# The ones beside the values written by GpSimd in place of ScalarE, in the opening of a one-core transformer block

## The chip, the cores and the metric

The kernel runs on one core of one Trainium2 chip. The metric is the device time of one execution in microseconds (us), measured as medians over several runs. All timed runs quoted here are in the fast state (granted TensorE clock 0.998 to 1.0), except one single run (e8) whose state is unknown and which is used for its trace alone. Where a ratio is quoted, it is the mean time of one kernel's fast runs over the mean of the other's fast runs of the same rounds, so it is not quite the ratio of the medians.

The engines are called TensorE (PE in the profile, PEld for its weight loads), VectorE (DVE), ScalarE (ACT) and GpSimd (POOL); SP issues most of the transfers.

## The reference

A block of 2048 rows by 512 columns: attention with 32 heads of 16, then a gated unit of width 1792, each behind a layer norm.

```python
x = A_x
h = x + _A_ref(_layernorm(x, axis=-1), A_wqkv, A_wo)
h2 = h + _B_ref(_layernorm(h, axis=-1), B_w_gate, B_w_up, B_w_down)
return h2
```

## The kernel before

The kernel fixes the order of every engine's instructions itself. In the opening it loads the first 512 rows (four row tiles of 128), takes each tile's mean and variance, normalises and transposes them, projects the first queries and keys, and then starts the exponentials, which go on until 696 us. The attention sums come from a column of constants beside each head's 16 values: `Vaug` has 17 columns per head, and the last one must be filled once ("the ones" below; the value written is 0.5). That is 16 row tiles x 32 heads = 512 elements of 2 bytes in each partition, 34 bytes apart. Some names recur: the ramp is a row of the numbers 0 to 31, from which VectorE makes the identity matrix that TensorE transposes with; the masks pick out single heads, and the mask scaling multiplies one of them by a constant; the warming matmuls are products of `fill` that nobody reads, run while TensorE would otherwise wait.

```python
nc.vector.memset(eps_t[:], 1e-5)
nc.scalar.activation(out=A0[:], in_=eps_t[:], func=ACT.Sqrt)      # warms the table
fill = prep.tile([P, QC], BF16, name="fill")
nc.scalar.activation(out=Vaug[:, :, :, DH:VW], ...)               # the ones: 0.5 everywhere
nc.gpsimd.memset(fill[:], 1.0)                                    # for TensorE's warming matmuls
nc.gpsimd.memset(eps4_t[:], 4e-5)
nc.gpsimd.memset(power[:], -0.5)
ramp = prep.tile([P, 2, 32], BF16, name="ramp")
for k in range(32):
    nc.gpsimd.memset(ramp[:, 0, k:k + 1], float(k))               # VectorE makes the identity of it
nc.gpsimd.tensor_scalar(out=eps4_t[:], in0=eps4_t[:], scalar1=1.0, scalar2=None, op0=ALU.mult)
# ... cut: VectorE's identity and masks, then the tasks of the opening
def stats_task(c, i):
    def on_act():      # tile 1: mean and mean square by two activations on ScalarE
        ...
    # tiles 0, 2, 3: ln_stats on VectorE
def root(i):           # ScalarE: square root of the variance
    ...
def pool_rstd(c, i):   # later tiles: GpSimd makes the scale ...
    ...
def pool_apply(c, i):  # ... and the normalised rows that TensorE transposes
    ...
```

The `tensor_scalar` at the end of GpSimd's part multiplies by one: it changes nothing. It stands there so that GpSimd has run such an instruction once before its real work, which begins with the second group of row tiles.

Of the kernel before, what the change touches and what calls it, by code (L numbers as in the profile page):

```python
# [8 lines left out]
FP32 = mybir.dt.float32  # L9
# [6 lines left out]
ACT = mybir.ActivationFunctionType  # L16
# [130 lines left out]
def kernel(  # L147
# [11 lines left out]
    nc = tc.nc  # L159
    P = 128  # L160
    S, D = A_x.shape[1], A_x.shape[2]
    H, DH = 32, 16
    F = B_w_gate.shape[1]
    NT = S // P
# [19 lines left out]
    VW = DH + 1  # L184
# [21 lines left out]
    eps_t = const.tile([P, 1], FP32)  # L206
# [10 lines left out]
    Vaug = const.tile([P, NT, H, VW], BF16)  # L217
# [26 lines left out]
    for c in range(2, NQC):  # L244
# [5 lines left out]
    nc.vector.memset(eps_t[:], 1e-5)  # L250
    nc.scalar.activation(out=A0[:], in_=eps_t[:], func=ACT.Sqrt)
    fill = prep.tile([P, QC], BF16, name="fill")
    nc.scalar.activation(out=Vaug[:, :, :, DH:VW], in_=eps_t[:].to_broadcast([P, NT * H]).rearrange(
        "p (t h o) -> p t h o", t=NT, o=1), func=ACT.Copy, scale=0.0, bias=0.5)
    nc.gpsimd.memset(fill[:], 1.0)
    nc.gpsimd.memset(eps4_t[:], 4e-5)
    nc.gpsimd.memset(power[:], -0.5)
    ramp = prep.tile([P, 2, 32], BF16, name="ramp")
    for k in range(32):
        nc.gpsimd.memset(ramp[:, 0, k:k + 1], float(k))  # L260
    nc.gpsimd.tensor_scalar(out=eps4_t[:], in0=eps4_t[:], scalar1=1.0, scalar2=None, op0=ALU.mult)
    psp = main.enter_context(tc.tile_pool(name="psum", bufs=1, space=PSUM))
    PS = psp.tile([P, 8, QC], FP32, name="PS")
# [149 lines left out]
    for i in range(TQ):  # L413
# [5 lines left out]
            out=mv0[i][:, 2:3], in_=mv0[i][:, 2:3])))  # L419
# [6 lines left out]
    for h in range(2):  # L426
# [5 lines left out]
        out=small.tile([P, 1], FP32, name="warm")[:], in_=eps_t[:], func=ACT.Exp)))  # L432
# [18 lines left out]
    for word in START:  # L451
        t, eng = tasks[word[1:]], word[0]
# [1071 lines left out]
    while chain:  # L1524
# [8 lines left out]
    fill = [lambda i=i: nc.tensor.matmul(hps[i], lhsT=ident2[:], rhs=xl[:, i, :], start=True, stop=False)  # L1533
            for i in range(n)]
    fill += [lambda p=p, i=i: nc.tensor.matmul(hps[i], lhsT=OT[qc, p][:, i * P:(i + 1) * P], rhs=wo_sb[:, p, :],
                                               start=False, stop=False) for p in range(NP - 1) for i in range(n)]
    fill = deque(fill)
    nc.scalar.activation(out=small.tile([P, 1], FP32, name="warm")[:], in_=eps_t[:], func=ACT.Sqrt)
    tw = {}
    for i in range(QB):  # L1540
        t = dvx.tile([P, 3, GQ, QC], I16, name="J", bufs=QB)[:].rearrange("p a b n -> p (a b n)")
# [139 lines left out]
```

## Time and profile before

| | before |
|---|---|
| median of the 6 runs beside the changed kernel | 731.30 us (731.12 to 732.11) |
| span of the profiled run | 729.3 us |
| first large exponential begins | 12.68 us |
| GpSimd's first TENSOR_SCALAR begins | 11.55 us |
| GpSimd's first real work begins | 15.35 us |

The prediction shows the page, the chain of waits and the timeline of the opening. Five more lines of the timeline of the kernel before matter later. The columns of the timeline are start in us, length in us, engine, line, operation, output and input, shapes, count, and in brackets the idle time before it with what ended it.

```profile
4.93 0.89 ACT L364 ACTIVATE junk<-xb 128x512 bf16<-128x512 bf16 x1
...
7.55 0.40 PE L315 MATMUL PS<-ident_bf,xn 128*128 128x128 bf16 x4 [1.11 <-DVE xn L385]
...
12.68 8.36 ACT L1447 ACTIVATE pt<-PS 128x1024 f16<-128x1024 f32 x9 [0.50 <-PE PS L1067]
...
15.35 0.24 POOL L538 TENSOR_SCALAR nv<-mv 128x2 f32<-128x2 f32 x1 [3.54 <-DVE mv L284]
...
43.89 3.28 ACT L1447 ACTIVATE xb<-PS 128x1024 f16<-128x1024 f32 x3 [0.19 <-issue]
```

ScalarE begins the statistics of row tile 1 at 4.93 us, and the first large exponential at 12.68. TensorE waits 1.11 us for the first normalised rows. GpSimd is ready early and waits 3.54 us for VectorE before its first real work: that is its slack. And at 43.89 us ScalarE has a short idle time of 0.19 us that nothing in the profile explains ("issue").

### The profile page before, as it was taken

The page shows a single profiled execution, that of the slowest core. Times are in us where ns is not written, and L with a number is a line of the kernel's source. Part 1 is how long each engine was busy: PE and PEld are TensorE (multiplying, and loading weights), DVE is VectorE, ACT ScalarE, POOL GpSimd, SP SyncE. Part 2 cuts the span into 40 slices and gives each one's busy share as a digit, 9 for nine tenths or more (in the row PEclk, how much of TensorE's full clock was granted, in tenths as well). Part 3 has the DMA queues.
Part 4 walks back from the last instruction along what each step waited for, and adds up shares of the span by engine and source line. Part 5 has one row for each costly group of instructions (what it writes and reads, how often), then busy time and mean ns, then how long its engine had stood idle before and what let it go on. Part 6 is the DMA issues. An engine that isn't in the chain of part 4 may idle for free.

```text
span 729.3 us, 26553 instructions
## 1 busy us (share of the span) xinstructions
PE 712.6 (98%) x11169; PEld 335.7 (46%) x11169; DVE 664.1 (91%) x1299; ACT 702.0 (96%) x787; POOL 426.4 (58%) x728
## 2 busy tenths in 40 slices
PE   8999999999999999999999999999999999999997
PEld 3322224444454445544545454545554455445564
DVE  7989989999999998999999999989999999999952
ACT  8999999999999999999999999999999999999962
POOL 2725657775566755656656766566664665666610
PEclk9999999999999999999999999999999999999999
DMA  8300006000223013211224023301322133013450
GB/s 259 88 11 10 11 8 178 2 3 2 74 78 95 14 33 105 85 45 46 67 62 109 9 82 89 75 17 44 106 67 60 39 103 103 10 24 89 117 161 19
DMA packets 85741, 47.39 MB, mean 65 GB/s; under 512 B 17520, under 2 KB 85616, under 8 KB 85616
## 3 DMA queue, kind: packets, MB, share of 16 engines
q1 hardware_dynamic: 85328, 45.37, 22.1%
q8 instruction: 89, 1.46, 0.9%
q14 instruction: 36, 0.29, 0.1%
q10 hardware_dynamic: 288, 0.26, 0.1%
HBM read 37.75 MB, written 2.10 MB: 55 GB/s over the span
## 4 chain that ended last, share of the span: by engine, by line
PE 69%; ACT 20%; DVE 7%; issue 2%; DMA 1%; POOL 1%; SPq 0%; ACTq 0%; DVEq 0%; POOLq 0%
PE PS L1067 23%; PE PS L1235 20%; ACT pt L1447 13%; PE PS L803 12%; PE PS L821 6%; DVE J L1259 3%; PE PS L321 3%; ACT xnT L1447 2%; PE PS L326 2%; PE PS L746 2%; ACT xb L1447 1%; ACT th L833 1%; ACT QTb L1447 1%; POOL J L1280 1%; DMA out_dram<-ob 1%
## 5 line engine op out<-in xcount | busy, mean ns | idle before, releaser
L1280 POOL INT64_ADD J<-J x658 | 407.9, 632 | 253.5 <-DVE J L1259 207.2
L1447 ACT ACTIVATE pt<-PS 128x1024 f16<-128x1024 f32 (+2 forms) x523 | 519.9, 1117 | 2.9 <-PE PS L1067 2.4
L1259 DVE TENSOR_SCALAR J<-PS 128x512 int16<-128x512 f32 x626 | 411.5, 678 | 17.7 <-PE PS L1067 12.6
L1067 PE MATMUL PS<-QT,KT 32*128 32x256 bf16 (+1 forms) x3712 | 264.1, 276 | 8.6 <-ACT pt L1447 3.6
L1235 PE MATMUL PS<-J,Vaug 128*17 128x256 f16 (+1 forms) x3195 | 226.1, 279 | 0.5 <-DVE J L1304 0.3
L1235 PE MATMUL PS<-pt,Vaug 128*17 128x256 f16 (+1 forms) x2042 | 198.3, 279 | 0.0
L1067 PEld LDWEIGHTS <-KT 32*128 32x128 bf16 x3840 | 89.7, 92 | 204.3 <-issue 200.5
L1235 PEld LDWEIGHTS <-Vaug 128*17 128x17 bf16 x5841 | 131.5, 90 | 78.4 <-issue 73.6
L803 PE MATMUL PS<-xnT,wgu 128*128 128x256 bf16 x784 | 112.9, 275 | 0.0
L1447 ACT ACTIVATE xnT<-PS 128x1024 f16<-128x1024 f32 (+1 forms) x85 | 92.2, 1116 | 0.5 <-PE PS L1067 0.2
L1304 DVE TENSOR_TENSOR J<-J 128x1024 f16<-128x1024 f16 (+1 forms) x110 | 78.4, 713 | 12.7 <-POOL J L1280 12.2
L803 PEld LDWEIGHTS <-wgu 128*128 128x128 bf16 x784 | 63.8, 98 | 38.5 <-issue 32.7
L821 PE MATMUL PS<-wd,hT 128*128 128x512 bf16 x196 | 56.7, 384 | 0.0
L833 ACT ACTIVATE th<-PS 128x512 f32<-128x512 f32 (+1 forms) x63 | 38.8, 616 | 8.8 <-DVE hT L816 5.0
L1235 PE MATMUL PS<-xnT,Vaug 128*17 128x256 f16 x346 | 46.7, 274 | 0.0
L1447 ACT ACTIVATE QTb<-PS 128x1024 f16<-128x1024 f32 x40 | 44.0, 1100 | 0.0
L875 DVE SCALAR_TENSOR_TENSOR hT<-th,PS 128x512 bf16<-128x512 f32 x49 | 33.1, 676 | 0.8 <-PE PS L803 0.8
L1134 DVE STREAM_TRANSPOSE xs<-PS 128x256 f32<-128x256 f32 (+1 forms) x60 | 27.5, 458 | 1.7 <-PE PS L1235 1.4
L1105 DVE TENSOR_TENSOR o<-xs,rsum 128x128 bf16<-128x128 f32 (+1 forms) x60 | 24.5, 409 | 2.1
L1447 ACT ACTIVATE xb<-PS 128x1024 f16<-128x1024 f32 (+1 forms) x25 | 26.0, 1086 | 0.3 <-issue 0.2
L1235 PE MATMUL PS<-QTb,Vaug 128*17 128x256 f16 x160 | 25.7, 274 | 0.0
L1447 ACT ACTIVATE pe<-PS 128x1024 f16<-128x1024 f32 (+1 forms) x21 | 21.9, 1094 | 0.9 <-PE PS L1067 0.8
(126 smaller groups left out, 390.7 us busy)
## 6 DMA issues: line engine op xcount, KB each, us to landing
wgu<-in_B_w_gate_dram SPq DMA_DIRECT2D x49, 256.0 KB, 3.0
wgu<-in_B_w_up_dram SPq DMA_DIRECT2D x49, 256.0 KB, 3.4
out_dram<-ob SPq DMA_DIRECT2D x16, 128.0 KB, 1.7
QT<-qd SPq DMA_DIRECT2D x112, 16.0 KB, 1.8
wd<-in_B_w_down_dram SPq DMA_DIRECT2D x1, 1792.0 KB, 9.2
xr<-in_A_x_dram SPq DMA_DIRECT2D x14, 128.0 KB, 3.4
xb<-in_A_x_dram SPq DMA_DIRECT2D x6, 256.0 KB, 5.5
J<-in_B_w_gate_dram SPq DMA_DIRECT2D x4, 384.0 KB, 4.3
```

The lines of the kernel that those rows point to most:

```text
L803: nc.tensor.matmul(ps[:, 0:PARTS[r][2]].rearrange("p (i q) -> p i q", q=P), lhsT=w[:, d, :], rhs=hn_of(r)[:, :, d, :], start=(d == 0), sto ...
L821: nc.tensor.matmul(ps, lhsT=hT[:, f, i * P:(i + 1) * P], rhs=wd[:, f, :], start=(f == 0), stop=(f == FC - 1))
L833: nc.scalar.activation(out=th[:, 0:ps.shape[-1]], in_=ps, func=ACT.Tanh, scale=0.5)
L875: nc.vector.scalar_tensor_tensor(out=hT[:, f:f + k, 0:w], in0=th[f][:].rearrange("p (k n) -> p k n", k=k), scalar=1.0, in1=ps2.rearrange(" ...
L1067: nc.tensor.matmul(pss[:, ui, i * CW[qc]:(i + 1) * CW[qc]], lhsT=KT[g // 2][32 * j:32 * j + 32, k * P:(k + 1) * P], rhs=q[32 * j:32 * j + ...
L1105: nc.vector.tensor_tensor(out=o2[:, 0:w // 32, DH * a:DH * a + DH], in0=xs[:, 0:w // 32, 0:DH], in1=rec.to_broadcast([P, w // 32, DH]), op ...
L1134: j = dve(650 - ns[0], lambda: nc.vector.transpose(out=xs[:, 0:w // 32, :].rearrange("p b r -> p (b r)"), in_=src), LAST, st["xs"], pr=-1)
L1235: nc.tensor.matmul(dst[32 * j:32 * j + VW, 0:w], lhsT=un.v[:, kt * SPAN[qc] + i, h, :], rhs=un.ap[:, i * w:(i + 1) * w], start=clears and ...
L1259: nc.vector.tensor_scalar(out=J[:, 0, k, :], in0=src, scalar1=ZOFF, scalar2=float(-min(CHORDS)), op0=ALU.add, op1=ALU.max)
L1280: nc.gpsimd.int64_add(words(s), words(0), CHORDS[s - 1] * (1 + 2 ** 16 + 2 ** 32 + 2 ** 48))
L1304: nc.vector.tensor_tensor(out=f1, in0=f1, in1=J[:, 0, 0:k, :].bitcast(FP16), op=ALU.add)
L1447: ex = nc.scalar.activation(out=pt, in_=pss[:, 0:wa, :], func=ACT.Exp, scale=AS)
```

## The change

Its intent: ScalarE shall begin the statistics of row tile 1 as soon as the tile lands, and VectorE its own likewise. GpSimd takes over the ones, behind the ramp that VectorE waits for; and the fill is written as 256 fp32 words with the same bits, to be out of the ramp's way sooner.

```diff
     fill = prep.tile([P, QC], BF16, name="fill")
-    nc.scalar.activation(out=Vaug[:, :, :, DH:VW], in_=eps_t[:].to_broadcast([P, NT * H]).rearrange(
-        "p (t h o) -> p t h o", t=NT, o=1), func=ACT.Copy, scale=0.0, bias=0.5)
-    nc.gpsimd.memset(fill[:], 1.0)
+    nc.gpsimd.memset(fill[:].bitcast(FP32), 1.001937866210938)
     nc.gpsimd.memset(eps4_t[:], 4e-5)
     nc.gpsimd.memset(power[:], -0.5)
     ramp = prep.tile([P, 2, 32], BF16, name="ramp")
     for k in range(32):
         nc.gpsimd.memset(ramp[:, 0, k:k + 1], float(k))
+    nc.gpsimd.memset(Vaug[:, :, :, DH:VW], 0.5)
     nc.gpsimd.tensor_scalar(out=eps4_t[:], in0=eps4_t[:], scalar1=1.0, scalar2=None, op0=ALU.mult)
```

## The prediction

> **What bounds the kernel now.** I first read the page, to see which engine limits the whole run.
>
> ```profile
> PE 712.6 (98%) x11169; PEld 335.7 (46%) x11169; DVE 664.1 (91%) x1299; ACT 702.0 (96%) x787; POOL 426.4 (58%) x728
> PE 69%; ACT 20%; DVE 7%; issue 2%; DMA 1%; POOL 1%; SPq 0%; ACTq 0%; DVEq 0%; POOLq 0%
> ```
>
> The first line is busy time per engine in a span of 729.3 us, the second the chain of work that ended last. The reader is to see a program with TensorE and ScalarE (ACT) full nearly to the end. Such a middle part leaves little to win, and the change touches nothing in it. What it touches lies before the first large exponential (ACT, line 1447, at 12.68 us), so I then read the chain of waits in order of time over the first 24 us. Its columns are start and length in us, and the work.
>
> ```profile
> 1.64 1.28 ACT L251
> 2.92 0.01 issue
> 2.93 0.20 ACT warm L251
> 3.13 2.26 ACT Vaug L253
> 5.40 0.52 ACT junk L364 x2
> 5.92 0.02 issue
> 5.94 0.72 ACT junk L366 x2
> 6.66 0.19 ACT QT L381
> 6.86 0.02 issue
> 6.88 0.17 DVE QT L418
> 7.05 0.03 issue
> 7.08 0.41 DVE xn L385
> ```
>
> The write of the 512 ones (Vaug L253) is on the chain with 2.26 us. It delays ACT's statistics of row tile 1 (L364, L366), these the first square root (L381), and that VectorE's (DVE's) reciprocal (L418) and normalised rows (L385), which everything later waits for. Last I read the timeline of all engines over the same stretch.
>
> ```profile
> 0.73 0.52 POOL L255 MEMSET fill<- 128x512 bf16 x1 [0.29 <-POOLq L1665]
> 1.25 1.12 POOL L260 MEMSET ramp<- 128x1 bf16 x32
> 1.31 5.13 PE L448 MATMUL PS<-fill 128*128 128x512 bf16 x13 [1.31 <-POOL eps_t L256]
> ...
> 2.41 0.21 DVE L266 STREAM_TRANSPOSE ramp<-ramp 128x32 bf16<-128x32 bf16 x1 [1.45 <-POOL ramp L260]
> ...
> 3.71 0.17 DVE L274 TENSOR_SCALAR maskz<-mask 128x2 f32<-128x2 f32 x1
> 3.79 0.69 DVE L281 BATCH_NORM_STATS2 st<-xb 128x6 f32<-128x512 bf16 x1
> ...
> 6.88 0.16 DVE L418 RECIPROCAL QT<-QT 128x1 f32<-128x1 f32 x1 [1.40 <-ACT QT L381]
> ...
> 11.55 0.26 POOL L261 TENSOR_SCALAR eps_t<-eps_t 128x1 f32<-128x1 f32 x1 [9.17 <-issue]
> ```
>
> DVE sits idle for 1.40 us before its first reciprocal, because of ACT; and its first statistics follow its mask work without a gap, 0.08 us after that work's last start. The transfers of the opening, asked for narrow stretches, give issue to landing: tile 0 is issued at 0.73 and takes 3.0 us (lands at 3.73); tile 1 takes 2.8 (3.53); tiles 2 and 3 are issued near 1.2 and take 3.2 and 2.9 (about 4.4 and 4.1). So DVE already starts almost at the landing of tile 0, while ACT starts tile 1 at 4.93, 1.4 us after it landed.
>
> **What the Trainium skill says.** "SBUF — State Buffer", the note on cachelines under "Door 1: The DMA port swizzle": accesses within one 16-byte line go at full rate, each crossing to a new line costs. The ones lie 17 bf16 elements, 34 bytes, apart, so every element is a new line. The trace agrees for ACT: 512 strided elements took 2.36 us, while the same kind of write of 512 elements into a dense PSUM row (line 430) took 0.61. Whether GpSimd (POOL) pays this, no row of before shows. "GPSIMD Engine Reference", section 3.1, gives 1.03 cycles per element for the simplest bodies: 512 x 1.03 / 1.2 GHz = 0.44 us; the trace agrees, 0.46 us from the start of fill's memset to the next start (0.73 to 1.19). Its section 2.1 says that the first call of a freshly loaded kernel hides a load of about 6 us that no row shows; the trace has 9.17 us of "issue" before POOL's first TENSOR_SCALAR, which I read as this, at a different size. "SBUF — State Buffer", section "Who interferes with whom": POOL and DVE share one port pair, which a two-port DVE instruction takes for its whole length; no wait of before's opening shows such a block.
>
> **The change part by part.**
> *Fill as fp32 words.* The 512 bf16 become 256 fp32, the same bits. At 0.46/512 us each, half of them saves 0.23 us of POOL ahead of the ramp. Ramp, DVE's transpose and masks, and TensorE's warming matmuls all come 0.23 earlier. For DVE the statistics cannot come before tile 0 at 3.73: gain there about 0.05 us, to about 3.75. TensorE's 13 fills end near 6.2 in place of 6.44.
> *ACT's write goes.* The warm square root runs from 2.93 to 3.13, tile 1 lands at 3.53, so its statistics begin near 3.56. In the trace, the activation of line 366 needs 0.54 us to its read of the accumulator and 0.63 to the next ACT work; the first pass needs about 0.75 alike (0.54 and the 0.21 from 5.73 to 5.94). So the first root starts at 3.56 + 0.75 + 0.63 = 4.94 in place of 6.57, 1.63 earlier. It needs DVE's statistics of tile 0, done at about 4.65, so it needn't wait. Its result reaches DVE 0.31 later (6.57 to 6.88 now), at 5.25.
> *The next wait.* DVE must by then have finished tile 2, which it takes before the reciprocal: that ends at 5.30 + 0.18 = 5.48 now and about 5.45 after. So the reciprocal starts near 5.45 and not 5.25: DVE gains 6.88 - 5.45 = 1.43 us, its whole idle time and no more. This is the term I choose as the gain.
> *What follows.* The normalised rows start near 5.65; TensorE's transpose, 0.46 later now (7.08 to 7.54), could start at 6.1 but stands behind the fills to 6.2, so it gains about 1.3. Four warming matmuls and the first projection then come near 7.36 (8.65 now); its weights, issued at 1.67 and 2.16 with 4.3 and 4.4 us, land at 6.0 and 6.6, no limit. The second transpose (9.13 now) depends on DVE and can gain the 1.43. ACT's table load for the exponentials, 8.93 now, comes near 7.64 and still ends before the copy that follows needs it. First exponential: about 12.68 - 1.4 = 11.3 us.
> *The memset of the ones.* It starts near 2.15 on POOL, after the ramp. If strides are free it lasts 0.45 us; at ACT's rate 2.3, to 4.4. Its readers come late: the scaling of Vaug (DVE, 15.87 now) and the first products with it (TensorE, 16.87 now).
> *The sum at the end.* Behind the first exponential the order on every engine is unchanged. The later weights wv, wq and wk land at about 9.5, 14.0 and 15.4, well before their uses (wv at 13.44 now, wk's projection at 25.17), so the shift should be passed to the end. I take 1.35 of the 1.43, for a little loss in later waits: 731.24 - 1.35 = 729.89, say 729.9 us.
>
> **The rivals.**
> First, *POOL blocks DVE*: if the memset holds the shared pair until 4.4, the small mask scaling (near 3.5) waits, statistics start near 4.4, tile 2 ends near 6.1, and the gain is 6.88 - 6.1 = 0.8 us: 730.4. For it speaks ACT's own slow strided write; against it, that the mask scaling has two elements and may not use the second port. I give it one chance in five.
> Second, *POOL becomes late*: if the 9.17 us count from the end of the memset, POOL is ready at 4.4 + 9.2 + 0.3 = 13.9 in the slow case. Its first real work starts at 15.35 now, so about 13.95 after: no slack left. In the quick case it is ready near 12.1. A further 1 us here could stall TensorE's transposes of the next rows (18.91 now, about half a us after their rows were written). Then most of the gain would go: 730.5 to 731.2. One chance in ten.
> Third, *the gain is swallowed*: some later transfer or a drift between engines takes up the shift. Against it: TensorE's waits from 12.6 to 700 us sum up to only a few us, nearly all on ACT or DVE, which shift along, and 0.7 us on one transfer that this core issues itself.
> Fourth, *the gain stops at 0.23 us*, the fill alone, if ACT's write was not the limit; the chain above speaks against it.
>
> **Range and chances.** The main line gives 729.9; blocking or a late POOL gives 730.4 to 731; a full gain of 1.6, which would need DVE faster too, gives 729.6. The three runs of before span 0.9 us (731.21 to 732.11), two of them within 0.03. So 729.3 to 730.9 should hold it eight times in ten. Two per cent is 14.6 us, more than the whole opening of 12.7 us: within 2% is all but certain.
>
> **What would show it.** Right: ACT's first statistics near 3.56, DVE's idle before the first reciprocal gone, the first root near 4.94 and reciprocal near 5.45, the first exponential near 11.3, DVE's first statistics at about 3.75, and Vaug off the chain. Wrong: DVE's mask scaling or statistics starting past 4 us beside a long POOL memset (first rival); POOL's TENSOR_SCALAR ending past 14 us, with waits for POOL behind it (second); an early first exponential with an unchanged end (third). The prediction fails above all if the memset is far longer than ACT's 2.4 us, or if the shift is lost behind 12 us.

## The result, and the profile after

The median went from 731.30 to 730.41 us (six runs each; 730.12 to 731.64 after). The ratio is 0.9988 with a 95% interval of 0.9975 to 1.0001: within 2%, and on these runs alone not even clearly apart from no change. The lines below have numbers lower by one in the changed kernel (L1447 is L1446 there).

The page of the changed kernel, the two lines that answer to those of before:

```profile
PE 702.4 (96%) x11111; PEld 335.8 (46%) x11169; DVE 663.9 (91%) x1299; ACT 700.2 (96%) x786; POOL 429.0 (59%) x729
PE 62%; ACT 23%; DVE 6%; issue 4%; DMA 2%; SPq 1%; POOL 1%; DVEq 0%; ACTq 0%; POOLq 0%
```

ScalarE has one instruction fewer (786 for 787) and 1.8 us less work, GpSimd one more and 2.6 us more. TensorE's 10 us less are no gain: 58 matmul records are missing from this trace (11111 for 11169), and the weight loads are all there. The timeline of its opening:

```profile
0.73 0.31 POOL L253 MEMSET fill<- 128x256 f32 x1 [0.29 <-POOLq L1664]
...
2.10 2.27 POOL L259 MEMSET Vaug<- 128x512 bf16 x1
2.20 0.21 DVE L265 STREAM_TRANSPOSE ramp<-ramp 128x32 bf16<-128x32 bf16 x1 [1.24 <-POOL ramp L258]
...
3.41 0.63 ACT L363 ACTIVATE junk<-xb 128x512 bf16<-128x512 bf16 x1 [0.28 <-DMA xb<-in_A_x_dram]
3.51 0.88 DVE L273 TENSOR_SCALAR maskz<-mask 128x2 f32<-128x2 f32 x1
3.60 0.79 DVE L280 BATCH_NORM_STATS2 st<-xb 128x6 f32<-128x512 bf16 x1
...
4.79 0.28 ACT L380 ACTIVATE QT<-QT,eps_t 128x1 f32<-128x1 f32 x1
...
5.34 0.13 DVE L417 RECIPROCAL QT<-QT 128x1 f32<-128x1 f32 x1
...
5.98 0.40 PE L314 MATMUL PS<-ident_bf,xn 128*128 128x128 bf16 x4
...
11.10 3.77 ACT L1446 ACTIVATE pt<-PS 128x1024 f16<-128x1024 f32 x4 [0.50 <-PE PS L1066]
...
14.40 0.37 POOL L260 TENSOR_SCALAR eps_t<-eps_t 128x1 f32<-128x1 f32 x1 [10.04 <-issue]
14.85 0.24 POOL L537 TENSOR_SCALAR nv<-mv 128x2 f32<-128x2 f32 x1
```

ScalarE now waits for the transfer itself and starts at 3.41 us in place of 4.93; VectorE's wait of 1.40 us before the reciprocal is gone, and the reciprocal starts at 5.34 in place of 6.88. The first large exponential starts at 11.10 in place of 12.68, 1.58 us earlier. But GpSimd's TENSOR_SCALAR has moved from 11.55 to 14.40, and its real work follows at 14.85 without the slack of before. Two waits of the changed kernel show what came of it; the first line is from the waits of TensorE between 12 and 40 us (us in total, times, longest), the second from the timeline of ScalarE.

```profile
PE PS L692 <- POOL xn L544: 0.2, 1, 0.2
```

```profile
42.98 3.28 ACT L1446 ACTIVATE xb<-PS 128x1024 f16<-128x1024 f32 x3 [0.50 <-issue]
```

In the kernel before, TensorE had no wait for GpSimd in that stretch, and ScalarE's idle time there was 0.19 us.

To see where the shift is lost, take the 688 activations of 1024 or 1536 columns, which come in the same order in every kernel, and subtract the start of the same one in the trace of before. A negative number is a kernel ahead of it.

| activation (start before) | 1st (12.68) | 11th (21.94) | 26th (38.80) | 31st (45.71) | last (694.82) |
|---|---|---|---|---|---|
| changed kernel | -1.58 | -1.21 | -1.21 | -0.90 | -1.08 |

So the opening gained 1.58 us; 0.37 went by 21.94 us and 0.31 between 38.8 and 45.7 us. After that the shift moves between -1.2 and -0.6 us, and the two traces end 1.08 us apart, against 0.89 us between the medians. The experiments are about the two losses.

One view misleads here. The chain of waits of the changed kernel over its first 24 us runs so:

```profile
7.29 0.04 issue
7.33 7.81 DMA wk_sb<-in_A_wqkv_dram
15.15 0.03 POOLq L544
15.17 0.74 POOL rstd L538
```

It lays GpSimd's lateness on the transfer of `wk_sb`, because an update of that transfer came just before. But L538 reads only what L537 wrote and the constant `power`, and GpSimd's rows stand back to back from 14.40 us on. In e2 below the same instruction starts at 14.29 us, while the transfer lands only near 15.4 there (issued at 7.71, 7.7 us to landing). The releaser is inferred from what ended last, and this one is a coincidence. What held GpSimd is in its own row: 10.04 us of idle time before the TENSOR_SCALAR.

### The profile page after: what moved, and what is told of

Same layout as the page of the kernel before. It is cut to its first block, busy times and chain, and to the rows that moved or that the text cites. A ratio compares the mean times of both kernels' runs of the same rounds, so it can differ in the third digit from the quotient of the medians.

```text
span 728.3 us, 26497 instructions
## 1 busy us (share of the span) xinstructions
PE 702.4 (96%) x11111; PEld 335.8 (46%) x11169; DVE 663.9 (91%) x1299; ACT 700.2 (96%) x786; POOL 429.0 (59%) x729
## 4 chain that ended last, share of the span: by engine, by line
PE 62%; ACT 23%; DVE 6%; issue 4%; DMA 2%; SPq 1%; POOL 1%; DVEq 0%; ACTq 0%; POOLq 0%
PE PS L1066 21%; PE PS L1234 18%; ACT pt L1446 17%; PE PS L802 11%; PE PS L820 5%; DVE J L1258 3%; PE PS L320 3%; ACT xnT L1446 3%; PE PS L325 1%; ACT QTb L1446 1%; DMA wk_sb<-in_A_wqkv_dram 1%; PE PS L745 1%; ACT th L832 1%; ACT xb L1446 1%; PE PS L1640 1%
## 5 line engine op out<-in xcount | busy, mean ns | idle before, releaser
L1446 ACT ACTIVATE pt<-PS 128x1024 f16<-128x1024 f32 (+2 forms) x523 | 519.9, 1115 | 3.1 <-PE PS L1066 2.2
L1066 PE MATMUL PS<-QT,KT 32*128 32x256 bf16 (+1 forms) x3712 | 263.9, 276 | 13.9 <-ACT pt L1446 5.7
L1446 ACT ACTIVATE xnT<-PS 128x1024 f16<-128x1024 f32 (+1 forms) x85 | 92.2, 1117 | 0.4 <-PE PS L1066 0.2
L820 PE MATMUL PS<-wd,hT 128*128 128x512 bf16 x167 | 50.2, 383 | 3.5 <-issue 3.5
L1446 ACT ACTIVATE QTb<-PS 128x1024 f16<-128x1024 f32 x40 | 44.0, 1100 | 0.0
L1446 ACT ACTIVATE xb<-PS 128x1024 f16<-128x1024 f32 (+1 forms) x25 | 26.0, 1084 | 0.6 <-issue 0.5
L1446 ACT ACTIVATE pe<-PS 128x1024 f16<-128x1024 f32 (+1 forms) x21 | 21.8, 1092 | 0.9 <-PE PS L1066 0.8
```

Of the source, the lines that this page charges most:

```text
L820: nc.tensor.matmul(ps, lhsT=hT[:, f, i * P:(i + 1) * P], rhs=wd[:, f, :], start=(f == 0), stop=(f == FC - 1))
L1066: nc.tensor.matmul(pss[:, ui, i * CW[qc]:(i + 1) * CW[qc]], lhsT=KT[g // 2][32 * j:32 * j + 32, k * P:(k + 1) * P], rhs=q[32 * j:32 * j + ...
L1446: ex = nc.scalar.activation(out=pt, in_=pss[:, 0:wa, :], func=ACT.Exp, scale=AS)
```

## The experiments

Eleven runs were made, of nine new kernels, the changed one again and e7 again; all gave correct results. The table has them together, with the shifts as above. "Idle" is the idle time before GpSimd's first TENSOR_SCALAR, "TS" its start.

| kernel | idle | TS | 1st | 11th | 26th | 31st | last | median (runs) | ratio to before |
|---|---|---|---|---|---|---|---|---|---|
| before | 9.17 | 11.55 | 0 | 0 | 0 | 0 | 0 | 731.30 (6) | |
| changed | 10.04 | 14.40 | -1.58 | -1.21 | -1.21 | -0.90 | -1.08 | 730.41 (6) | 0.9988 |
| after_again | 9.67 | 14.03 | -1.52 | -1.52 | -1.53 | -1.22 | -1.70 | 730.42 (5) | 0.9984 |
| e1_fill_only | 8.54 | 10.71 | 0.00 | 0.00 | -0.01 | -0.01 | +0.22 | 731.45 (4) | 1.0000 |
| e2_ones_behind_load | 8.58 | 10.74 | -1.38 | -1.38 | -1.34 | -1.04 | -1.68 | 729.72 (5) | 0.9977 |
| e3_ones_on_dve | 8.45 | 10.61 | -0.96 | -0.96 | -0.97 | -0.66 | -0.37 | 730.84 (5) | 0.9986 |
| e4_mask_late | 11.39 | 15.76 | -1.63 | +0.10 | +0.10 | +0.41 | -0.10 | 731.16 (4) | 0.9990 |
| e5_ones_twice | 9.55 | 16.25 | -0.65 | +0.59 | +0.58 | +0.95 | +1.00 | 732.12 (4) | 1.0004 |
| e6_ones_split | 7.86 | 10.59 | -1.64 | -1.64 | -1.52 | -1.21 | -1.59 | 730.29 (4) | 0.9982 |
| e7_act_count | 8.52 | 10.68 | -1.45 | -1.45 | -1.41 | -1.41 | -1.60 | 729.61 (5) | 0.9970 |
| e8_dense_delay | 12.53 | 17.00 | +0.01 | +1.31 | +1.30 | +1.38 | +1.52 | 732.59 (1) | |
| e9_after_act_count | 9.32 | 13.70 | -1.57 | -1.56 | -1.57 | -1.50 | -1.77 | 729.59 (5) | 0.9973 |
| e10_best_again | 7.60 | 9.76 | -1.65 | -1.65 | -1.60 | -1.52 | -1.91 | 729.21 (6) | 0.9970 |

The kernel before, beside these, had medians of 731.57 (e1, e2, e4, e5), 731.77 (after_again, e3, e6, e7) and 731.53 (e8, e9, e10). All shifts are against the one trace of the kernel before. after_again, e3, e6 and e7 ran on one chip, the other experiments on another.

My theory at the start: ScalarE's write was the limit of the opening, and GpSimd's new work makes it late for TensorE. The rival: something else took the gain, such as a fixed time of GpSimd or drift.

### e1_fill_only: the fill alone

```diff
-    nc.gpsimd.memset(fill[:], 1.0)
+    nc.gpsimd.memset(fill[:].bitcast(FP32), 1.001937866210938)
```

> Only the fill as 256 fp32 words; ScalarE still writes the ones. Theory (ScalarE's write was the limit): VectorE's masks about 0.22 us earlier, but ScalarE's statistics still at about 4.9 us and the first large exponential at 12.6 to 12.7 us, so the end is within 0.1 us of the kernel before (731.3). Rival (the ramp in front of VectorE was the limit): the first exponential about 0.2 us earlier, near 12.45, and the end likewise.

Measured: the first exponential is where it was (shift 0.00), the ratio 1.0000 (0.9985 to 1.0015). Its timeline has VectorE's masks 0.20 us earlier, and ScalarE's first root unmoved:

```profile
3.51 0.17 DVE L274 TENSOR_SCALAR maskz<-mask 128x2 f32<-128x2 f32 x1
...
6.57 0.46 ACT L381 ACTIVATE QT<-QT,eps_t 128x1 f32<-128x1 f32 x2
```

So the fill gives nothing by itself; the opening's gain needs ScalarE's write to go.

### e2_ones_behind_load: the ones behind GpSimd's first TENSOR_SCALAR

```diff
-    nc.gpsimd.memset(Vaug[:, :, :, DH:VW], 0.5)
     nc.gpsimd.tensor_scalar(out=eps4_t[:], in0=eps4_t[:], scalar1=1.0, scalar2=None, op0=ALU.mult)
+    nc.gpsimd.memset(Vaug[:, :, :, DH:VW], 0.5)
```

> The changed kernel with the memset of the ones behind GpSimd's first TENSOR_SCALAR. Theory (the idle time before that instruction counts from the memset's end, and GpSimd's lateness gives back part of the gain): TENSOR_SCALAR at about 2.1 + 9.2 = 11.3 us, memset 11.6 to 13.9, first real GpSimd work near 14.0 in place of 14.85, no wait of TensorE for GpSimd's rows at 18 us, and the shift of the exponentials stays near 1.5 us at 40 us in place of 0.9 to 1.2. The mask scaling takes 0.17 us again in place of 0.88. End about 729.9 to 730.1. Rival (the load comes at a fixed time or the loss behind 12 us is something else): TENSOR_SCALAR still near 14 us or the shift drops to 1.2 us at 20 us as before; end 730.4.

Measured, in its timeline:

```profile
10.74 0.26 POOL L259 TENSOR_SCALAR eps_t<-eps_t 128x1 f32<-128x1 f32 x1 [8.58 <-issue]
10.96 2.27 POOL L260 MEMSET Vaug<- 128x512 bf16 x1
13.96 0.25 POOL L537 TENSOR_SCALAR nv<-mv 128x2 f32<-128x2 f32 x1 [0.74 <-DVE mv L283]
```

The TENSOR_SCALAR comes 8.58 us after the ramp, the memset fits into the hole behind it, and GpSimd waits for VectorE again (0.74 us) in place of the other way round. Nothing is lost between the 1st and the 11th exponential. The time is 729.72 us, the ratio 0.9977 (0.9963 to 0.9990). The first exponential gained only 1.38 here, 0.20 less than in the changed kernel: TensorE's 13 warming matmuls took 5.73 us in this trace and 5.01 in the other, so the first transpose began at 6.62 and not at 5.98. The instructions are the same. The warming matmuls start 0.40 to 0.43 us apart at first; in the changed kernel the last two of the 12 intervals are 0.22 and 0.21, in after_again the last three 0.22 to 0.27, and in e2 none is under 0.40. So when TensorE goes over to its faster rate differed from run to run.

### e4_mask_late: the small mask scaling out of the memset's way

```diff
 def masks():
     nc.vector.tensor_reduce(out=mask[:], ...)
-    nc.vector.tensor_scalar(out=maskz[:], in0=mask[:], scalar1=ZS, scalar2=None, op0=ALU.mult)
...
 def fix(c, i):
     mv = mv0[i]
+    if i == 1:
+        nc.vector.tensor_scalar(out=maskz[:], in0=mask[:], scalar1=ZS, scalar2=None, op0=ALU.mult)
```

> The changed kernel with VectorE's mask scaling (two elements) moved behind the first normalised rows, out of the time of GpSimd's memset. Theory (the small mask scaling takes two ports and waits for the memset, and the statistics end behind it): statistics of tile 0 end near 4.26 in place of 4.39, first reciprocal near 5.2 in place of 5.34, first exponential near 11.0 in place of 11.10; end the same as the changed kernel (730.4), since GpSimd is late all the same. Rival (the statistics themselves are slowed by the memset, or wait for the rows): statistics still end at 4.39 and the reciprocal stays at 5.34.

Measured:

```profile
3.60 0.69 DVE L279 BATCH_NORM_STATS2 st<-xb 128x6 f32<-128x512 bf16 x1
...
5.22 0.13 DVE L418 RECIPROCAL QT<-QT 128x1 f32<-128x1 f32 x1
...
15.76 0.26 POOL L260 TENSOR_SCALAR eps_t<-eps_t 128x1 f32<-128x1 f32 x1 [11.39 <-issue]
```

The next line is from the waits of TensorE between 12 and 45 us.

```profile
PE PS L693 <- POOL xn L545: 1.5, 2, 1.1
```

The statistics end at 4.29 in place of 4.39 and the reciprocal starts at 5.22 in place of 5.34: the block behind the memset is real, and worth 0.12 us there and 0.05 at the first exponential. What I had not expected is the second half: the same memset is followed by 11.39 us of idle time here, TensorE waits 1.5 us for GpSimd's rows, and the whole gain of the opening is gone by the 11th exponential (+0.10). Nothing in this edit touches GpSimd. So the idle time varies from run to run, and the loss with it; the four timed runs spread from 730.17 to 731.44 us.

### e5_ones_twice: the memset doubled

```diff
+    nc.gpsimd.memset(Vaug[:, :, :, DH:VW], 0.5)
     nc.gpsimd.memset(Vaug[:, :, :, DH:VW], 0.5)
```

> The changed kernel with the memset of the ones done twice, same values. Theory (lateness of GpSimd goes to the end nearly one to one): second memset ends at 6.6 us, TENSOR_SCALAR near 16.7 us in place of 14.40, first exponential still at 11.1 us, but TensorE waits some 2.3 us more for GpSimd's rows near 18 to 20 us, end about 732 to 732.7. Rival (GpSimd's time in the opening is hidden): end within 0.3 us of 730.4. Rival (load at a fixed time): TENSOR_SCALAR at 14.4 us as in the changed kernel.

Measured: TENSOR_SCALAR at 16.25 us, and the end 732.12 us, as the theory has it. It was wrong on the first exponential, which gained only 0.65: the second memset also held VectorE.

```profile
4.43 2.28 POOL L260 MEMSET Vaug<- 128x512 bf16 x1
...
5.52 1.33 DVE L385 TENSOR_SCALAR xn<-xb,QT 128x512 bf16<-128x512 bf16 x1
```

The normalising of the first rows, 0.41 us elsewhere, took 1.33 and ended just after the memset did (6.71 us). From the 1st to the 11th exponential another 1.24 us went.

### after_again: the changed kernel once more

No edit.

> The changed kernel itself once more, for a second trace on this chip. Theory (the idle time before GpSimd's first TENSOR_SCALAR varies from run to run, 8.5 to 11.4 us seen so far, and only beyond about 9.3 us does it delay TensorE): that idle time differs from the 10.04 us of the first trace, and the shift of the exponentials at 20 us is about 1.58 less the excess over 9.3 us; times spread by more than 0.5 us. Rival (fixed load): idle time again 10.0 us, shift 1.2 us at 20 us, spread under 0.3 us.

Measured:

```profile
14.03 0.26 POOL L260 TENSOR_SCALAR eps_t<-eps_t 128x1 f32<-128x1 f32 x1 [9.67 <-issue]
```

The idle time is 9.67 us and nothing is lost by the 11th exponential; its five runs span 729.40 to 730.85 us, the ratio is 0.9984 (0.9970 to 0.9998). The same program loses 0.37 us in one trace and nothing in another. The threshold of 9.3 us that I had expected was wrong: by it 0.37 us should have gone here too.

### e3_ones_on_dve: the ones on VectorE, before the ramp arrives

```diff
     nc.vector.memset(ident_bf[:], 0.0)
+    nc.vector.memset(Vaug[:, :, :, DH:VW], 0.5)
...
-    nc.gpsimd.memset(Vaug[:, :, :, DH:VW], 0.5)
```

> The changed kernel with the ones written by VectorE in its idle time before the ramp (0.96 to 2.20 us). Theory (a strided write of 2-byte elements costs every engine near 4.4 ns each, as ScalarE 2.36 us and GpSimd 2.27 us for 512): memset 2.3 us, transposed ramp only at about 3.2 us, statistics from about 4.6 us in place of 3.6, first exponential about 12.0, end about 730.7 to 731.0. Rival (VectorE writes one element per cycle at any stride): memset 0.6 us, hidden; TENSOR_SCALAR of GpSimd near 10.7 us, first exponential near 11.0 to 11.3, end 729.5 to 729.9, as good as the ones behind the load.

Measured:

```profile
2.66 0.48 DVE L264 MEMSET Vaug<- 128x512 bf16 x1 [1.70 <-issue]
2.78 0.39 DVE L265 STREAM_TRANSPOSE ramp<-ramp 128x32 bf16<-128x32 bf16 x1
```

The row says 0.48 us, but 1.70 us of unexplained idle time stand before it, and the profile shows nothing that the memset waits for: VectorE was free at 0.96 us and the row ends at 3.14. If the memset began at 0.96, it took about 2.2 us, 4.3 ns for each element, which is close to GpSimd's 4.4 (2.27 / 512). That is inferred: a memset of 0.48 us that began late for a reason the profile doesn't show would leave the same row. The transposed ramp is done 0.76 us later than in the changed kernel (3.17 for 2.41), and the first exponential gains 0.96 in place of 1.58. The end, 730.84 us, is in the theory's range. Whichever it was, VectorE is no better place.

### e6_ones_split: a quarter of the ones early, the rest behind the load

```diff
-    nc.gpsimd.memset(Vaug[:, :, :, DH:VW], 0.5)
+    nc.gpsimd.memset(Vaug[:, 0:TQ, :, DH:VW], 0.5)
     nc.gpsimd.tensor_scalar(out=eps4_t[:], ...)
+    nc.gpsimd.memset(Vaug[:, TQ:NT, :, DH:VW], 0.5)
```

> The changed kernel with the ones of row tiles 0 to 3 (128 elements) behind the ramp and the other 384 behind GpSimd's first TENSOR_SCALAR. Theory: first part 128 x 4.4 ns = 0.57 us (2.1 to 2.7), over before the mask scaling at 3.5, which takes 0.17 us; TENSOR_SCALAR near 2.7 + 8.6 to 9.3 = 11.3 to 12.0 us; second part 1.7 us, done by 13.8; no wait of TensorE for GpSimd at 18 us; end as with all behind the load, 729.6 to 730.0. Rival (load fixed in time or the memset's length is an overhead per instruction): first part over 1 us, mask scaling blocked, end 730.3.

Measured:

```profile
2.10 0.64 POOL L259 MEMSET Vaug<- 128x128 bf16 x1
10.59 0.26 POOL L260 TENSOR_SCALAR eps_t<-eps_t 128x1 f32<-128x1 f32 x1 [7.86 <-issue]
10.81 1.73 POOL L261 MEMSET Vaug<- 128x384 bf16 x1
```

The time goes with the number of elements, the mask scaling is not held (0.17 us), and the trace loses nothing by the 11th exponential. Its median, 730.29 us, is worse than expected, though the profiled run (729.51) is not; the three timed rounds (730.26 to 730.62) have no trace, so what happened in them stays open.

### e8_dense_delay: GpSimd late, and nothing else changed

This is e1 with a dense memset that nobody needs, of about the same length, while ScalarE still writes the ones.

```diff
+    nc.gpsimd.memset(Vaug2[:, 0:5], 0.5)
     nc.gpsimd.tensor_scalar(out=eps4_t[:], ...)
```

> The kernel before with the fill as fp32 words and one extra dense memset of 2720 2-byte elements (into a tile that is overwritten later) on GpSimd behind its ramp; ScalarE writes the ones. It asks what lengthens the idle time before GpSimd's first TENSOR_SCALAR (8.5 us behind the bare ramp, 9.55 to 11.4 behind the strided memset of the ones). Theory (a later start of it meets the busy transfers of the opening): dense memset 2.4 us, idle again 9.5 us or more, TENSOR_SCALAR past 14 us. Rival (it is the strided memset itself): idle about 8.5 us, TENSOR_SCALAR near 13.1 us. Mask scaling: blocked again (about 0.9 us) if any long memset of GpSimd does it.

Measured:

```profile
2.10 2.37 POOL L261 MEMSET Vaug<- 128x2720 bf16 x1
...
3.51 0.97 DVE L275 TENSOR_SCALAR maskz<-mask 128x2 f32<-128x2 f32 x1
...
17.00 0.26 POOL L262 TENSOR_SCALAR eps_t<-eps_t 128x1 f32<-128x1 f32 x1 [12.53 <-issue]
```

(The profile leaves out the number in `Vaug2`.)

The first exponential is where it was (+0.01), the 11th is 1.31 us late: GpSimd's lateness alone does it. A dense memset (2.37 us for 2720 elements, 0.87 ns each) holds VectorE's mask scaling as the strided one does, and the idle time behind it is the longest of all. So, as far as this one trace tells, it needs no stride to be that long.

The four traces with a loss agree on one rule. Take the start of TENSOR_SCALAR after the first exponential, less what was lost by the 11th: 14.40 - 11.10 - 0.37 = 2.93 (changed), 15.76 - 11.05 - 1.73 = 2.98 (e4), 16.25 - 12.02 - 1.24 = 2.99 (e5), 17.00 - 12.69 - 1.30 = 3.01 us (e8). Up to about 2.95 us after the first exponential GpSimd's first TENSOR_SCALAR is hidden (after_again: 2.88, no loss); beyond that, in these four, each us is lost.

### e7_act_count: one small activation put back on ScalarE

All kernels without ScalarE's write up to here lost 0.30 to 0.37 us between the 26th and the 31st activation, with 0.50 us or more of idle time at the same row; before and e1 did not. What they share is one instruction fewer on ScalarE. So e7 is e2 with a tiny activation in the old place, where ScalarE would wait for its rows anyway.

```diff
     nc.scalar.activation(out=A0[:], in_=eps_t[:], func=ACT.Sqrt)
+    nc.scalar.activation(out=A0[:], in_=eps_t[:], func=ACT.Copy, scale=0.0, bias=0.5)
```

> The ones behind the load, with one small ScalarE activation (128x1) put back where its write of the ones stood, so that ScalarE has as many instructions as before. Theory (the 0.31 us that every kernel without ScalarE's write lost near 43 us, idle time 0.50 in place of 0.19 with no releaser shown, comes from where that instruction stands in ScalarE's stream): idle time 0.19 again and the shift is the same at 38 and at 46 us; end 0.3 us earlier than the ones behind the load, about 729.4. Rival (it comes from absolute time or from other engines): idle time 0.50 again, end 729.7.

Measured:

```profile
42.48 3.28 ACT L1447 ACTIVATE xb<-PS 128x1024 f16<-128x1024 f32 x3 [0.19 <-issue]
```

The idle time is 0.19 us again and the shift is the same at the 26th and the 31st (-1.41). The median is 729.61 us, all five runs lie within 0.45 us (729.25 to 729.70), and the ratio is 0.9970 (0.9956 to 0.9983). An instruction more made the kernel no slower; its median is 0.1 us ahead of e2's where 0.3 was expected, on another chip and by less than the spread of e2's runs, so the trace carries this, not the time.

### e9_after_act_count and e10_best_again

e9 is the changed kernel with the small activation put back. e10 is e7 again.

> The changed kernel with one small ScalarE activation (128x1) in the place of the removed one, and the memset of the ones where the change put it. Theory: the 0.31 us near 43 us is saved (idle 0.19), the lateness of GpSimd stays (idle before its TENSOR_SCALAR 9.5 to 11 us): end about 730.1, with a spread over 0.5 us. Rival (the end hangs on the opening alone): 730.4 as the changed kernel.

> The same kernel as e7_act_count (ones behind the load, ScalarE count restored) once more beside the others. Theory: 729.6 again, spread under 0.5 us, idle before GpSimd's TENSOR_SCALAR near 8.5 us, TensorE never waits for GpSimd near 18 us. Rival (e7 was lucky): 730 or more, or a spread like the changed kernel's.

Measured, in e9 and then in e10:

```profile
13.70 0.26 POOL L261 TENSOR_SCALAR eps_t<-eps_t 128x1 f32<-128x1 f32 x1 [9.32 <-issue]
...
42.39 3.28 ACT L1447 ACTIVATE xb<-PS 128x1024 f16<-128x1024 f32 x3 [0.26 <-issue]
```

```profile
9.76 0.26 POOL L260 TENSOR_SCALAR eps_t<-eps_t 128x1 f32<-128x1 f32 x1 [7.60 <-issue]
...
42.37 3.28 ACT L1447 ACTIVATE xb<-PS 128x1024 f16<-128x1024 f32 x3 [0.27 <-issue]
```

e9 has 729.59 us, ratio 0.9973 (0.9960 to 0.9987), better than expected and with a spread of only 0.56 us; its idle time before TENSOR_SCALAR was 9.32 us, its start 2.59 us after the first exponential, so hidden. ScalarE's idle time near 42 us was 0.26, and 0.07 us of shift went there. e10 has 729.21 us (729.02 to 730.08 in six runs), ratio 0.9970 (0.9957 to 0.9982), with the TENSOR_SCALAR at 9.76 us. Its spread, 1.06 us, is over the 0.5 expected, and the idle time 0.9 us under the 8.5 expected. Against the median of before on that chip, 731.53 us, the version with the ones behind the load and the small activation is 2.3 us faster, the fastest kernel. Beside the changed kernel it ran on one chip only: e7's five runs there (729.25 to 729.70 us) lie below four of after_again's five. How much of its lead over e9 is the place of the memset and how much is luck in the idle time is not settled: e9 and e10 ran in the same rounds, 0.38 us apart with overlapping spreads.

## Why the prediction was right or wrong

The time was right: 730.41 us against 729.9 with a range of 729.3 to 730.9. The gain was 0.89 us where the main line had 1.35, because the term for what is passed on to the end was mis-sized. That the median lies in the range owes something to luck: e4, with the same instructions on GpSimd but 11.39 us of idle time, ended at 731.44 us in its profiled run and had a median of 731.16, both outside it.

**What bounds the opening** was right. ScalarE's write was on the chain; without it the wait of VectorE vanished. e1 shows that the fill alone gives nothing. The lengths of the steps were right too: from the start of ScalarE's statistics to the first root it took 4.79 - 3.41 = 1.38 us, as summed (0.75 + 0.63); both came 0.15 us earlier than predicted, because tile 1 was there by 3.41 us.

**The fill** saved 0.21 us of GpSimd (next start at 0.98 in place of 1.19), 0.23 expected.

**The next wait** was right in kind: VectorE's tile 2, not ScalarE's root, sets the reciprocal. The gain there was 6.88 - 5.34 = 1.54 and not 1.43. I had let the reciprocal start at the end of the row before it; in the trace it starts 0.08 us before that end (5.24 + 0.18 = 5.42). TensorE's first transpose gained 7.55 - 5.98 = 1.57 where 1.3 was summed. The first exponential came at 11.10 (11.3 expected), a gain of 1.58.

**The memset of the ones** took 2.27 us, the slow of the two cases. The prediction's note from "SBUF — State Buffer" on 16-byte lines fits: 4.6 ns per strided element on ScalarE (2.36 / 512) and 4.4 on GpSimd, against 0.9 dense on GpSimd (0.46 / 512). No run varies the stride, so that the lines are the reason is not shown.

**"The sum at the end"** is the step that failed in size: "I take 1.35 of the 1.43, for a little loss in later waits". In place of 0.08 us, 0.68 of the 1.58 was lost by 45.7 us in the profiled run: 0.37 behind GpSimd, and 0.31 at one ScalarE instruction that no view before had pointed to. The rest was passed on: after 46 us the shift stayed between -1.2 and -0.6 us, so the third rival, a gain swallowed by drift or transfers, did not happen.

**The rival of a late GpSimd** came true in part, with one chance in ten given to it: its sign, a TENSOR_SCALAR ending past 14 us (14.77) with waits for GpSimd behind it, is there, but 0.37 us went there where it said most of the gain (in e4's trace all of it went). Its arithmetic said 13.9 us for GpSimd and "no slack left"; measured were 13.96 to 16.02 (the end of TENSOR_SCALAR), after 9.3 to 11.4 us of idle time in place of a fixed 9.2, in the four traces that have this one memset in this place (changed kernel, after_again, e4, e9). What I had missed is that the idle time is no constant. That is shown by e4 against e9, which ran on one chip with the same instructions on GpSimd (11.39 and 9.32 us), and by the changed kernel against itself (10.04 and 9.67). Why it is mostly longer when it begins at 4.4 us or later (9.3 to 12.5) than between 2.1 and 2.8 (7.6 to 9.2) isn't shown; the transfers of the opening are denser later (165 GB/s over the first 5 us of the changed kernel, 337 and 349 over the next two stretches of 5), but no run separates that. I read it, as in the prediction, as the hidden first-call load of "GPSIMD Engine Reference", section 2.1. No row shows the load itself. But that section measures it from a row MODIFY_POOL_CONFIG, and two such rows of GpSimd's queue stand at the line of this TENSOR_SCALAR in every trace, shortly before or after the last memset ends (4.04 and 4.08 us in the changed kernel).

**The rival of a blocked VectorE** came true in mechanism and not in size. The mask scaling of two elements took 0.88 us, to 4.39, just past the memset's end at 4.37, which fits "SBUF — State Buffer", section "Who interferes with whom": `tensor_scalar` is among the operations that can enter a two-port mode, and then it contends with GpSimd, and the one that comes second waits for the whole of the other. e5 and e8 show it too, and e4 by its absence. But the statistics behind it had begun at 3.60 and ended together with it, so 0.12 us were lost at the reciprocal and not 0.6.

**The fourth rival**, a gain of 0.23 from the fill alone, is ruled out by e1.

**The 0.31 us near 43 us** were in no rival. e7 shows that they come and go with one ScalarE instruction 40 us earlier; e9 and e10 agree, less 0.07 and 0.08 us. Through what stays open, but the traces tell one thing more. The instruction queue q14 carries one packet of 8 KB near this row: it begins 1.1 to 1.2 us before the row in the six traces with the full count of ScalarE instructions, and 0.65 to 0.70 us after it in the seven with one fewer. So the count moves an instruction packet against the row; yet in the seven it begins after the idle time has ended, so its landing is not what ended it.

## What to carry to other kernels

Before you move work to an idle engine, ask what that engine does next and how far ahead of its consumer it is: GpSimd's 9 to 11 us of hidden idle time behind the memset turned 2.27 us of "free" work into a loss of up to 1.7 us. Put such work behind a slow first instruction rather than before it, if what it writes is needed late: in e2, e7 and e10 nothing was lost that way by the 11th exponential. When a kernel is this full, follow one row through both traces and subtract the starts; the places where the difference jumps are the losses, whatever the summed waits say.

## What the Trainium skill lacked or had wrong

- "GPSIMD Engine Reference", section 2.1, gives about 6 us for the hidden load at a first call. If that is what stands before the first TENSOR_SCALAR (the two MODIFY_POOL_CONFIG rows speak for it), it took 7.60 to 12.53 us here, and varied for one and the same program (10.04 and 9.67 us).
- "SBUF — State Buffer", note on cachelines, gives no size for the penalty, and no page I read has one for strided writes. Here it was 4.4 ns for each 2-byte element 34 bytes from the last on GpSimd (2.27 us for 512) and 4.6 on ScalarE (2.36 us), against 0.9 dense on GpSimd.
- "VectorE: DVE Perf Modes", section "Zero memsets can be issued as uint32 (trn2)", says that a memset takes one cycle per element whatever the dtype; with the 34-byte stride of e3 it ended 2.18 us after VectorE came free, where 512 elements at that rate and the page's 0.96 GHz give an estimate of 0.53 us. Its row shows 0.48 us; whether the 1.70 us of idle time before it belong to the memset isn't shown, and no page I read settles it.
- "Runtime: NRT & Kernel Launch", section "Instruction fetch mechanics", calls the cost of crossing to the next block of instructions mostly hidden. Here 0.31 us of ScalarE idle time with no releaser came and went with one earlier instruction (0.50 against 0.19 us); no run shows that it is a fetch, and no page I read has another account of it.
